# A fused recurrent-attention and expert kernel: the first group's down-projections move behind the second group's attention

## The chip, the cores and the metric

The kernel runs on one core of a Trainium2 chip. The core has five engines that run their own instruction queues in order: TensorE (PE in the profile, with its weight loads as PEld), VectorE (DVE), ScalarE (ACT), GpSimd (POOL) and SyncE (SP), which here only starts DMAs. They meet through semaphores. The metric is the device time of one execution in microseconds. Of the kernel before, three runs took 387.95, 388.36 and 388.54 us; the median is 388.36.

## The reference

Two blocks follow one another. The first is a gated linear recurrence over 768 steps for 4 batches of 8 heads with 48 dimensions:

```python
for t in range(S):
    state = alpha[:, :, t, :, None] * state + np.einsum('bhd,bhe->bhde', k[:, :, t], v[:, :, t])
    y[:, :, t] = np.einsum('bhd,bhde->bhe', q[:, :, t], state)
```

Its output becomes 3072 tokens of 384 values, and goes through an expert block with 1024 hidden values:

```python
h = x @ w_in
h_max = np.max(h, axis=-1, keepdims=True)
e = np.exp(h - h_max)
sm = e / (np.sum(e, axis=-1, keepdims=True) + 1e-09)
solu = h * sm
mu = np.mean(solu, axis=-1, keepdims=True)
var = np.mean((solu - mu) ** 2, axis=-1, keepdims=True)
ln = (solu - mu) / np.sqrt(var + 1e-06) * g_ln
return (ln @ w_out).astype(np.float32)
```

The two weights arrive as 64-bit floats, the rest as 32-bit floats.

## The kernel before

The 768 steps are six groups (g) of 128 steps of all four batches, 512 tokens each. A group goes through three stages.

Attention. Alpha is turned so that time lies along the rows (`alpha_T`, or `turned` on TensorE for the first groups), a backward scan over it gives the decay from a step to the group's end (`scan_back`, tile hT), a forward scan gives the decay from the start (`scan_on`, tile aT, seeded with the inverse of the first). A test that alpha lies in range goes over the same data on ScalarE (`alpha_over`). Keys and queries are multiplied with these decays (`keys`, `queries`), and then scores, masked scores (`masked`, tile sT), the reading of the state (`read_state`), the reading of the values (`read_values`) and the new state (`next_state`) are matmuls and their evictions. `move_lasts` and `move_firsts` bring the queries into the layout of the state by 12 small DMAs, and `decay` multiplies the state by what a group decays it. The tiles of scores, of the transposed keys, of y and of the state's increment all use the four PSUM banks a0 to a3.

Up. For each of eight blocks f of 128 hidden values, three matmuls give h (`up_mm`, PSUM pool of two banks), ScalarE takes its exponential, VectorE the product u = h e, ScalarE the square of u (`up_act`). The sums over the hidden values of e and of u squared are kept by running sums over f (`running`: GpSimd for e, VectorE for the squares); for group 0 they are made on TensorE instead, by matmuls with ones that place four blocks in four quarters of a bank (`array_sums`). `token_sums` turns them into one number for each token. No maximum is subtracted.

Down. For each batch n of a group, four matmuls over f = 0 to 3 and four over f = 4 to 7 (`down(n, half)`), then the normalization from the sums (`finish`). w_out is scaled by g_ln's row, and centred by its column mean (`mean`, `centre`), so that the mean of solu needs no pass of its own. Group 0's downs use w_out before it is centred, and `finish` adds the correction.

The weights come in eight pieces of 64-bit data (0 to 3 of w_in, 4 to 7 of w_out, two blocks f each). `fetch` loads a piece into one of six slots of `room`, `bits` turns it into 32-bit floats by five VectorE steps, `in_range` tests it by two ScalarE passes, and `scaled` multiplies w_out's rows by g_ln on ScalarE. The slots also hold u: three for even groups, three for odd ones, so that a raw piece must be used before u takes its slot.

The order is written out by hand: instructions go to each engine's queue in the order of the program (`tc.manual_schedule`). First group 0's attention (L673 to L710), then a loop over f for group 0's ups with the conversion of pieces 2 to 6 between them (L712 to L742), then a passage with group 0's downs, the rest of the conversion, the mean of w_out and group 1's attention (L743 to L811). From there on each period g does the ups of group g, the downs of group g - 1 (from a list `todo`), and the attention of group g + 1, at places s = 0 to 7 that a table gives (`usual`, and `first` for g = 1, L815 to L826). Before the change `todo` is empty in period 1, and `centres` (L880) puts the centring of w_out at places 4, 6 and 7 of it.

Where a word for the periods is needed: the first period reaches from group 0's first up to group 1's first up, the second from there to group 2's first up, the third to group 3's.

Of the kernel before, what the change touches and what calls it, by code (L numbers as in the profile page):

```python
# [9 lines left out]
FP = mybir.dt.float32  # L10
# [6 lines left out]
P = 128  # L17
# [15 lines left out]
def fast_path(ctx, tc, q, k, v, alpha, moe_w_in, moe_w_out, moe_g_ln, out):  # L33
# [46 lines left out]
    small_ones = const.tile([P, 32], FP, name="small_ones")  # L80
# [33 lines left out]
    seed = [const.tile([P, NP, SW], FP, name=f"seed{i}") for i in range(2)]  # L114
# [95 lines left out]

    def scan_on(g, i):
        part = slice(NP * i, NP * i + NP)
        s = seed[i % 2]
        if i == 2:
            nc.vector.tensor_copy(out=fend[:, g], in_=h4[:, :, 1])

        least = small.tile([P, NP, 1], FP, name="least")
        nc.vector.tensor_scalar(out=least, in0=h4[:, part, 1:2], scalar1=LEAST, scalar2=None, op0=ALU.max)  # L218
        nc.vector.reciprocal(out=s[:, :, 0:1], in_=least)
        scan(aT[:, part], aT[:, part], s, False)  # L220
# [175 lines left out]
    def up_act(g, f):  # L396
        d = gr[g]
        h = d["h"]
        if g:
            e, u2 = (ring.tile([P, T4], FP, name=x) for x in ("e", "u2"))  # L400
        else:
            e, u2 = (sT[:, f % 4, 4 * i : 4 * i + 4].rearrange("p b t -> p (b t)") for i in range(2))
        u = u_of(g, f)
        nc.scalar.activation(out=e, in_=h, func=AF.Exp)  # L404
        nc.vector.tensor_tensor(out=u, in0=h, in1=e, op=ALU.mult)  # L405
        nc.scalar.activation(out=u2, in_=u, func=AF.Square)  # L406
        d[f] = e, u2

    def running(g, f):
# [9 lines left out]
        for i, eng in enumerate((nc.gpsimd, nc.vector)):  # L419
# [4 lines left out]
    def array_sums(g, half):  # L424


        d = gr[g]
        if half == 0:
            d["q"] = [ps_a.tile([P, T4], FP, tag=f"a{i}", name=f"quarters{i}") for i in range(2)]
        for i in range(2):  # L430
            for f in range(4):
                r = quarter(f)
                nc.tensor.matmul(
                    d["q"][i][r], lhsT=ones[:, 0:32], rhs=d[4 * half + f][i], start=half == 0, stop=half == 1,
                    tile_position=(0, r.start), skip_group_check=True,
                )
        if half:
            d["p"] = one.tile([P, 2, T4], FP, name="p")
            for i in range(2):
                nc.scalar.copy(out=d["p"][:, i], in_=d["q"][i])  # L440
            d["unit"] = small_ones
# [6 lines left out]
    def token_sums(g):  # L448
# [3 lines left out]
        t = ps_a.tile([P, B, 2, 32], FP, tag="a3", name="rows") if g else ps_h.tile([P, B, 2, 32], FP, tag="h", name="rows")  # L452
# [131 lines left out]
    def bits(i, part=None):  # L584
        if not float64:
            return
        lo, hi = raws[i][:, :, :, 0], raws[i][:, :, :, 1]
        if part != 1:
            made[i] = [
                lots[2 * (i % 2) + x].rearrange("p (c f) -> p c f", c=hi.shape[1]) for x in range(2)  # L590
            ]
            top = made[i][0].bitcast(U32)
# [6 lines left out]
        if part != 0:  # L599
            top, low = made.pop(i)  # L600
            nc.vector.tensor_scalar(
                out=low.bitcast(U32), in0=top.bitcast(U32), scalar1=0xFF800000, scalar2=None, op0=ALU.bitwise_and
            )
            nc.vector.scalar_tensor_tensor(out=low, in0=lo, scalar=2.0**-52, in1=low, op0=ALU.mult, op1=ALU.mult)
            nc.vector.tensor_tensor(out=place(i), in0=low, in1=top, op=ALU.add)
# [13 lines left out]
    def mean(half):  # L619


        m = ps_h.tile([P, 512], FP, tag="h", name="sums")[:, 0:DM]
# [33 lines left out]
    for s in seed:  # L656
        nc.gpsimd.memset(s, 0.0)
# [6 lines left out]
    nc.vector.memset(small_ones, 1.0 / 32)  # L664
# [16 lines left out]
    alpha_over(0)  # L681
    scan_on(0, 2)
# [28 lines left out]

    for f in range(FC):  # L712
        up_mm(0, f)
        if f == 4:
            array_sums(0, 0)
        up_act(0, f)

        for half in (0, 1) if f == 0 else (f + 1,):
            bits(2 + half // 2, half % 2)
        if f == 0:  # L720
            next_state(0)
            fetch(4, 3)
            load_first(k, kn, 1)
            load_first(q, qn, 1)
            load(alpha, an, 1)
        elif f == 1:
            in_range(2)
        elif f == 2:
            ends_k = ends_of(kn, "e")
        elif f == 3:  # L730
            in_range(3)
            fetch(5, 1)
            fetch(6, 2)
            ends_q = ends_of(qn, "u2")
        elif f == 5:
            in_range(4)
            fetch(7, 3)
            load_v(1)
        elif f == 6:
            scaled(4)  # L740
        elif f == 7:
            scaled(5)  # L742
    bits(6, 1)  # L743
    tk = three("tp_k", [(ps_a, "a2"), (ps_a, "a3"), (ps_h, "h")])
    turned(kn, ends_k, tk)
    load(k, kn, 2)
    array_sums(0, 1)
    down(0, 0)
    scaled(6)
    bits(7)  # L750
    token_sums(0)
    alpha_T(1)
    down(1, 0)
    scaled(7)
    tq = three("tp_q", [(ps_a, "a0"), (ps_a, "a1")])
    turned(qn, ends_q, tq, range(H))
    in_range(5)
    in_range(6)
    for i in range(3):
        scan_back(1, i)  # L760
        part = slice(NP * i, NP * i + NP)
        nc.vector.tensor_tensor(out=kT[:, part], in0=tk[i], in1=hk[:, part], op=ALU.mult)
    mean(0)
    down(0, 1)
    mean(1)
    alpha_over(1)
    load(alpha, an, 2)
# [642 lines left out]
```

## Time and profile before

| what | us |
|---|---|
| median of three runs | 388.36 |
| the profiled execution, its own time | 388.88 |
| its span in the profile | 387.1 |
| first up of group 0 | 32.47 |
| first up of group 1 | 111.87 |
| first up of group 2 | 151.36 |
| first up of group 3 | 206.95 |
| first up of group 4 | 264.12 |

Times in the profile count from the start of the span. In its lists of groups, a line gives the source line, the engine, the operation, the tiles written and read, the shape and the count, then the busy time and the mean of one, then the idle time ahead of it with what ended it. In the timeline a line begins with its start and its length, and merges like instructions that follow one another. Matmuls appear as two records each, since a 32-bit matmul makes two passes. The chain that ended last is only the last output's eviction (VectorE and ScalarE, after 382.34 us), so the reading goes by stretches of time. Clocks are shares of TensorE's full speed that were granted.

### The profile page before, as it was taken

The page shows a single profiled execution, that of the slowest core. Times are in us where ns is not written, and L with a number is a line of the kernel's source. Part 1 is how long each engine was busy: PE and PEld are TensorE (multiplying, and loading weights), DVE is VectorE, ACT ScalarE, POOL GpSimd, SP SyncE. Part 2 cuts the span into 40 slices and gives each one's busy share as a digit, 9 for nine tenths or more (in the row PEclk, how much of TensorE's full clock was granted, in tenths as well). Part 3 has the DMA queues.
Part 4 walks back from the last instruction along what each step waited for, and adds up shares of the span by engine and source line. Part 5 has one row for each costly group of instructions (what it writes and reads, how often), then busy time and mean ns, then how long its engine had stood idle before and what let it go on. Part 6 is the DMA issues. An engine that isn't in the chain of part 4 may idle for free. (4 is left out here: it accounts for less than half of the span.)

```text
span 387.1 us, 10060 instructions
## 1 busy us (share of the span) xinstructions
PE 365.6 (94%) x4341; PEld 219.3 (57%) x4341; DVE 250.7 (65%) x413; ACT 144.5 (37%) x255; POOL 111.5 (29%) x122
## 2 busy tenths in 40 slices
PE   8798899988979998999999999998999999999994
PEld 8685335656645556555557555665556565555652
DVE  0989878996997858885584875664875413444600
ACT  2628566681415426134253153342142132222100
POOL 6000000000232992437130466210475211323200
PEclk9989999999989999999999999999999999999999
DMA  9891978248355535717142627003123000000011
GB/s 182 166 323 51 221 220 200 47 97 183 92 131 104 116 79 102 147 35 161 37 105 47 140 62 172 13 11 70 36 63 89 22 16 8 23 21 20 22 44 47
DMA packets 72439, 36.05 MB, mean 93 GB/s; under 512 B 48185, under 2 KB 69953, under 8 KB 72385
## 3 DMA queue, kind: packets, MB, share of 16 engines
q1 hardware_dynamic: 71360, 34.39, 37.6%
q10 hardware_dynamic: 1024, 0.92, 0.7%
q8 instruction: 36, 0.59, 0.7%
q14 instruction: 19, 0.15, 0.1%
HBM read 25.30 MB, written 4.72 MB: 78 GB/s over the span
## 5 line engine op out<-in xcount | busy, mean ns | idle before, releaser
L390 PE MATMUL h<-x,w_in 128*128 128x512 f32 x288 | 134.8, 608 | 3.4 <-DVE room L405 1.6
L501 PE MATMUL o<-w_out,room 128*128 128x385 f32 x384 | 133.1, 491 | 1.1 <-DVE least L218 1.1
L501 PEld LDWEIGHTS o<-w_out,room 128*128 128x128 f32 x384 | 71.6, 190 | 56.8 <-issue 15.3
L390 PEld LDWEIGHTS h<-x,w_in 128*128 128x128 f32 x288 | 53.1, 192 | 63.5 <-issue 49.2
L405 DVE TENSOR_TENSOR room<-h,e 128x512 f32<-128x512 f32 x40 | 27.7, 693 | 62.6 <-ACT e L404 62.6
L404 ACT ACTIVATE e<-h 128x512 f32<-128x512 f32 x40 | 23.9, 597 | 89.1 <-PE h L390 88.5
L421 POOL TENSOR_TENSOR p<-p,e 128x512 f32<-128x512 f32 x30 | 40.8, 1360 | 21.9 <-ACT e L404 21.5
L406 ACT ACTIVATE u<-room 128x512 f32<-128x512 f32 x40 | 25.2, 630 | 42.5 <-DVE room L405 42.5
L532 POOL TENSOR_TENSOR r<-sums,mhalf 128x1 f32<-128x1 f32 x20 | 12.5, 626 | 91.5 <-DVE sums L524 91.5
L291 DVE TENSOR_TENSOR sT<-a,mask 128x512 f32<-128x512 f32 x44 | 27.3, 683 | 15.3 <-PE a L280 15.3
L280 PE MATMUL a<-qv,kT 32*128 32x128 f32 x704 | 26.2, 289 | 3.9 <-DVE least L218 2.0
L280 PEld LDWEIGHTS a<-qv,kT 32*128 32x128 f32 x704 | 23.2, 196 | 11.0 <-issue 2.3
L421 DVE TENSOR_TENSOR p<-p,u 128x512 f32<-128x512 f32 x30 | 23.6, 786 | 8.4 <-ACT u L406 8.4
L204 DVE TENSOR_TENSOR_SCAN hT<-aT,unit 128x516 f32<-128x516 f32 x18 | 22.3, 1285 | 8.7 <-ACT aT L677 8.6
L204 DVE TENSOR_TENSOR_SCAN aT<-aT,seed 128x516 f32<-128x516 f32 x18 | 25.0, 1391 | 0.6
L329 PE MATMUL y<-sT,vn 128*32 128x128 f32 x768 | 22.6, 273 | 0.4 <-DVE sT L291 0.4
L329 PEld LDWEIGHTS y<-sT,vn 128*32 128x32 f32 x768 | 20.7, 110 | 2.9 <-issue 2.0
L228 POOL TENSOR_TENSOR kT<-kT,hT 128x1024 f32<-128x1024 f32 (+1 forms) x8 | 13.3, 1682 | 29.8 <-DVE kT L179 29.8
L359 ACT COPY x<-y 128x384 f32<-128x384 f32 x24 | 11.2, 480 | 22.7 <-PE y L329 22.7
L196 ACT ACTIVATE sq<-an,mone 128x1536 uint8<-128x1536 f32 x12 | 18.9, 1572 | 0.2
L243 POOL COPY qe<-hT 128x4 f32<-128x4 f32 x5 | 1.0, 191 | 59.4 <-DVE hT L204 59.4
L534 ACT ACTIVATE o_sb<-o,r 128x384 f32<-128x384 f32 x16 | 9.3, 581 | 17.2 <-POOL r L532 17.2
(142 smaller groups left out, 370.2 us busy)
## 6 DMA issues: line engine op xcount, KB each, us to landing
vn<-in_v_dram SPq DMA_DIRECT2D x24, 192.0 KB, 4.5
an<-in_alpha_dram SPq DMA_DIRECT2D x20, 192.0 KB, 4.1
out_dram<-o_sb SPq DMA_DIRECT2D x20, 192.0 KB, 2.0
room<-in_moe_w_in_dram SPq DMA_DIRECT2D x6, 512.0 KB, 7.5
room<-in_moe_w_out_dram SPq DMA_DIRECT2D x8, 384.0 KB, 4.3
kn<-in_k_dram SPq DMA_DIRECT2D x16, 192.0 KB, 3.9
qn<-in_q_dram SPq DMA_DIRECT2D x16, 192.0 KB, 4.7
lot<-qe SPq DMA_DIRECT2D x40, 64.5 KB, 2.1
```

The lines of the kernel that those rows point to most:

```text
L196: nc.scalar.activation(out=sq, in_=x, func=AF.Relu, scale=sign, bias=mone, accum_out=over[:, g, i : i + 1])
L204: nc.vector.tensor_tensor_scan(out=o, data0=a, data1=s, initial=1.0, op0=ALU.mult, op1=ALU.add)
L228: nc.gpsimd.tensor_tensor(out=kT[:, part], in0=kT[:, part], in1=hk[:, part], op=ALU.mult)
L280: nc.tensor.matmul(a[b][:, i], lhsT=kT[quarter(b), kb], rhs=qv[quarter(b), qb, 0:P], start=kb == h, stop=kb != h, tile_position=(32 * b, 0 ...
L291: nc.vector.tensor_tensor(out=sT[:, b, half * NP : half * NP + NP], in0=a[b], in1=mask[:, None, :].to_broadcast([P, NP, P]), op=ALU.mult,)
L329: nc.tensor.matmul(y_bank(b)[quarter(r), a], lhsT=lhsT, rhs=rhs, start=(b, r) not in begun, stop=stop, tile_position=(row, 32 * r), skip_g ...
L390: nc.tensor.matmul(h, lhsT=w_in[:, a, f * P : (f + 1) * P], rhs=d["x"][:, a].rearrange("p b t -> p (b t)"), start=(a == 0), stop=(a == KC ...
L404: nc.scalar.activation(out=e, in_=h, func=AF.Exp)
L405: nc.vector.tensor_tensor(out=u, in0=h, in1=e, op=ALU.mult)
L406: nc.scalar.activation(out=u2, in_=u, func=AF.Square)
L421: eng.tensor_tensor(out=p, in0=d[0][i] if f == 1 else p, in1=d[f][i], op=ALU.add)
L501: nc.tensor.matmul(d["o"][:, 0 : DM + 1], lhsT=u_of(g, f)[:, b * P : b * P + P], rhs=w_out[:, f], start=(f == 0), stop=(f == FC - 1), skip ...
```

## The change

- Group 0's downs leave the passage after the loop. They become the first `todo`, in the order of first halves of two batches, then their second halves, and are done in period 1. The sums and the mean of w_out follow them: `token_sums(0)` at place 0, `mean` at place 2.
- Group 1's keys and queries are turned on TensorE inside the loop over f, and copied from PSUM by ScalarE; their products with the decays are made by GpSimd from SBUF (`keys`, `queries`), not by VectorE from PSUM. Alpha's transposes, backward scans and range test of group 1 stand in the loop too, and the rest of its attention follows without downs.
- Of w_out, piece 4 is converted behind the first scores of group 1, piece 5 behind its state reads, pieces 6 and 7 at places 0 and 1 of period 1. The backward scans of group 3 move from the end of period 1 to place 0 of period 2 (`second`). The centring of w_out is at place 6 of period 1 (rows 0 to 3) and at place 0 of period 2 (rows 4 to 7).
- `bits` works in place in the weight, with one small tile beside it, and its last step is GpSimd's for pieces 3 to 7.
- One reciprocal for all twelve blocks of a group (`inverses`) takes the place of a clamp and a reciprocal for each of three parts; the copy of the group's ends is ScalarE's.
- Group 0's sum of e is a running sum on GpSimd, and its sum of squares a matmul sum after the loop (`array_squares`). Group 1's two running sums are both on GpSimd.

The instructions and transfers before group 0's first up are otherwise the same, except that the loads of group 1's alpha, keys and queries are issued before the loop.

```diff
-    seed = [const.tile([P, NP, SW], FP, name=f"seed{i}") for i in range(2)]
+    seed = const.tile([P, NB, SW], FP, name="seed")
...
+    def inverses(g):
+        nc.scalar.copy(out=fend[:, g], in_=h4[:, :, 1])
+        nc.vector.reciprocal(out=seed[:, :, 0:1], in_=h4[:, :, 1:2])
+
     def scan_on(g, i):
         part = slice(NP * i, NP * i + NP)
-        s = seed[i % 2]
-        if i == 2:
-            nc.vector.tensor_copy(out=fend[:, g], in_=h4[:, :, 1])
-
-        least = small.tile([P, NP, 1], FP, name="least")
-        nc.vector.tensor_scalar(out=least, in0=h4[:, part, 1:2], scalar1=LEAST, scalar2=None, op0=ALU.max)
-        nc.vector.reciprocal(out=s[:, :, 0:1], in_=least)
-        scan(aT[:, part], aT[:, part], s, False)
+        scan(aT[:, part], aT[:, part], seed[:, part], False)
...
-        for i, eng in enumerate((nc.gpsimd, nc.vector)):
+        for i, eng in enumerate((nc.gpsimd, nc.vector if g > 1 else nc.gpsimd)):
+            if g == 0 and i:
+                continue
...
+    def array_squares():
+        d = gr[0]
+        t = ps_a.tile([P, T4], FP, tag="a3", name="quarters")
+        for f in range(FC):
+            r = quarter(f % 4)
+            nc.tensor.matmul(
+                t[r], lhsT=ones[:, 0:32], rhs=d[f][1], start=f < 4, stop=f >= FC - 4,
+                tile_position=(0, r.start), skip_group_check=True,
+            )
+        nc.scalar.mul(out=d["p"][:, 1], in_=t, mul=1.0 / 32)
...
-            nc.vector.tensor_tensor(out=place(i), in0=low, in1=top, op=ALU.add)
+            eng = nc.vector if i < 3 else nc.gpsimd
+            eng.tensor_tensor(out=dst, in0=low, in1=dst, op=ALU.add)
...
     for f in range(FC):
+        up(0, f)
+        if f:
+            running(0, f)
         if f == 0:
+            bits(2, 0)
             next_state(0)
             fetch(4, 3)
         elif f == 1:
+            bits(2, 1)
             in_range(2)
         elif f == 2:
+            bits(3, 0)
+            ends_k = ends_of(kn, 1)
         elif f == 3:
+            bits(3, 1)
+            first_turned(
+                kn, ends_k, [(ps_a, "a0"), (ps_a, "a1"), (ps_a, "a2")], [kT[:, NP * i : NP * i + NP] for i in range(3)]
+            )
             in_range(3)
             fetch(5, 1)
             fetch(6, 2)
+            load_v(1)
+        elif f == 4:
+            alpha_T(1)
+            ends_q = ends_of(qn, 2)
+            load(k, kn, 2)
         elif f == 5:
+            scan_back(1, 0)
+            first_turned(
+                qn, ends_q, [(ps_a, "a3"), (ps_o, "o"), (ps_o, "o")],
+                [qv[:, 0:NP, 0:P], qv[:, NP:H, 0:P], qe[:, :, 0:P]],
+            )
+            load(q, qn, 2)
         elif f == 6:
+            scan_back(1, 1)
+            alpha_over(1)
+            load(alpha, an, 2)
         elif f == 7:
+            scan_back(1, 2)
+    inverses(1)
+    ends_of_decay()
+    keys(1)
     scan_on(1, 2)
+    queries(2)
+    move_lasts()
     apart()
+    array_squares()
+    scan_on(1, 0)
+    queries(0)
+    keys_back(1)
+    scan_on(1, 1)
+    queries(1)
     move_firsts()
     scores(1, 0)
+    bits(4)
+    in_range(4)
+    scaled(4)
+    fetch(7, 3)
     masked(0)
     scores(1, 1)
     masked(1)
+    decay(1)
     read_begin()
     read_state(0)
     read_state(1)
+    bits(5)
+    in_range(5)
+    read_values(1)
+    next_state(1)
+    scaled(5)
+    alpha_T(2)
     alpha_over(2)
     load(alpha, an, 3)
     for i in range(3):
         scan_back(2, i)
+    inverses(2)
...
-        behind={0: "v keys", 1: "on2 on0 on1", 2: "lasts firsts", 3: "apart", 5: "decay", 6: "alpha", 7: "back"},
+        behind={0: "v keys", 1: "on2 on0 on1", 2: "lasts firsts", 3: "apart", 5: "decay", 6: "alpha", 7: "next"},
...
     first = dict(
+        head={4: "keys_back", 5: "masked0", 6: "masked1"},
+        behind={0: "bits6 v keys", 1: "bits7 on2 on0", 2: "on1 lasts", 3: "firsts apart", 5: "decay", 7: "alpha"},
+        tail={2: "mean", 4: "scores0", 5: "scores1", 6: "begin read0", 7: "values"},
         middle={7: "read1"},
     )
+    second = dict(usual, behind={**usual["behind"], 0: "back v keys"})
...
-    centres = {4: (0, 1), 6: (2, 3), 7: (4, 5, 6, 7)}
-    todo = []
+    centres = {(1, 6): range(4), (2, 0): range(4, FC)}
+    todo = [(0, 0), (1, 0), (0, 1), (1, 1), (2, 0), (3, 0), (2, 1), (3, 1)]
...
-            if s == 0 and g > 1:
+            if s == 0:
                 token_sums(g - 1)
```

In the passage after the loop, the lines of the old order that only moved or went are left out of the diff above.

## The prediction

> **What bounds the kernel now.** I read the page's busy shares and slices, then a table of stretches cut at the first matmul of each group, then the timeline around the cuts.
>
> ```profile
> PE 365.6 (94%) x4341; PEld 219.3 (57%) x4341; DVE 250.7 (65%) x413; ACT 144.5 (37%) x255; POOL 111.5 (29%) x122
> ...
> PE   8798899988979998999999999998999999999994
> ...
> DVE  0989878996997858885584875664875413444600
> ```
>
> ```profile
> 32.47:63.50 31.03, 29.43 (x300) 13.48 (x302) 25.39 (x34) 20.19 (x41) 0.00 (x0) 1.00 0.77 190
> 63.50:111.87 48.37, 42.77 (x744) 27.69 (x737) 43.71 (x67) 24.30 (x44) 7.06 (x10) 1.00 0.52 116
> 111.87:151.36 39.49, 37.72 (x581) 22.15 (x573) 30.54 (x42) 17.57 (x31) 23.14 (x24) 0.96 0.41 95
> 151.36:206.95 55.59, 55.59 (x677) 33.01 (x669) 37.77 (x59) 19.43 (x33) 19.85 (x20) 1.00 0.44 97
> ```
>
> Columns of the second: length, then busy time of PE, weight load, DVE, ACT, POOL, clock, DMA. From 151.36 on TensorE never stops: the third period, 55.59 us, is one group's ups, attention and downs back to back. Up to 111.87 VectorE is the bound (43.71 of 48.37) and TensorE's downs stand beside it. The second period has no downs and takes 39.49; without them the third would take 55.59 - 8x2.57 - 0.65 = 34.4 (a half down steps every 2.57 us, the token sums are 0.65), so the second loses 5.1.
>
> ```profile
> 111.65 0.29 PE L367 MATMUL kv<-vn,kg 128*32 128x48 f32 x8 [2.49 <-issue]
> 111.87 9.69 PE L390 MATMUL h<-x,w_in 128*128 128x512 f32 x18
> ...
> 162.04 1.28 POOL L421 TENSOR_TENSOR p<-e 128x512 f32<-128x512 f32 x1
> ...
> 162.44 1.97 DVE L204 TENSOR_TENSOR_SCAN aT<-aT,seed 128x516 f32<-128x516 f32 x1
> ```
>
> Two prices. After a 2.49 us gap 18 up records took 9.69 us, where 427 ns each makes 7.69: a cold clock, 2.0 us. And a scan that alone takes 1.23 took 1.97, because a GpSimd sum held it till 163.3; GpSimd is held likewise (its two sums after 174.86 took 3.08 instead of 2.55). They take turns.
>
> **Bookkeeping.** The change takes 8 half downs (20.6), token sums (0.65) and the mean (1.2) out of the stretch before group 1's first up, and puts them behind it. Call that up's start t1 (now 111.87). With TensorE full, the second period becomes 55.59 + 1.2 = 56.8. Break-even: t1 + 56.8 = 151.36, so t1 = 94.6.
>
> **Start.** One reciprocal instead of three clamps and three reciprocals, and the copy of the ends to ScalarE, save VectorE 0.33, 0.41 and 0.48 us ahead of the scans (13.21 to 13.78, 16.70 to 17.11, 19.44 to 19.92). The query transposes land at 17.6 in any case, so half arrives: first up at 31.85, not 32.47.
>
> **First period.** VectorE loses half of w_out's conversion; ScalarE becomes the queue. From 35.3 it has eight exponentials and squares (8x1.13), two state copies 0.85, six copies of transposed keys and queries (6x0.58), two end copies 1.2, two range tests 4.0, and the alpha test 3.5, which stands ahead of the last exponential: 22.1. Each exponential waits for VectorE's product before its square, 8x0.75 = 6, and two waits for VectorE add some 2.4: last square 65.9, product 65.3. GpSimd takes the running sum of the exponentials (7x1.27) and piece 3's last step; it is idle from 22 to 80 in this trace, and the seventh up wants that piece only some 4 us after it is done. Alpha, keys and queries of group 1 are issued on SP ahead of w_out's pieces, at about 21 to 32, behind all of w_in's: they fit beside a DMA share of 0.30 at 30 to 40, and the pieces behind them wait for free slots in any case (SP waited up to 14.9 us for those).
>
> **Group 1's attention** is then bare: no downs beside it. Keys and queries, which were VectorE products from PSUM (5 or 6 x 0.69), become GpSimd ones: keys 2.18 + 1.18, queries 1.09 + 2x1.21, together 6.9, beside three scans of 1.2 on VectorE. If both run free, the last backward scan ends 66.5, the keys 70.1, the first queries 71.2, then apart 1.35, copy 0.57, four kg copies 1.75: 75. If they take turns, the last backward scan first waits for a sum (67.1), then scan, keys, scan, keys, scan and first queries follow one another from 67.4: 8.1, then the same 3.7: 79.2. Then nothing overlaps, since scores, masks and reads share four PSUM banks: scores 2.07, masks 2.48, scores 2.07, masks 2.48, state reads 2.4, values 3.7, key-values 1.5, hand-overs 0.5: 17.2. The decay needs 12 small DMAs after the queries (7.1 + 2.8 of issue in this trace) and falls just beside it; w_out's piece 7 is fetched behind those DMAs on SP, some 20 us ahead of its use. t1 = 92.2 to 96.4; I take the middle, 94.3: about break-even.
>
> **Second period.** Its second half downs, first wanted right after the third up, need w_out's pieces 6 and 7, whose conversion now stands in the queue behind much. On VectorE after t1: state sums 1.1, alpha's transposes 2.8, three scans 3.4, reciprocal 0.2, ends on ScalarE 0.2, exponential 0.6, product 0.6: 8.9. Token sums 1.1, four bit steps of piece 6 3.1: 13.1. The final sum is now GpSimd's: no row has 768 elements; between 1.24 for 512 and 2.18 for 1024, 1.7. Scaling 1.15: 15.9. ScalarE is in order, so the second exponential waits behind that scaling: 16.5, product 17.1. Piece 7's steps 3.1, sum 1.7, scaling 1.15: 23.1 free, 24.5 taking turns with the keys. TensorE reaches this down after 3 ups, 2 half downs and the token sums, 13.5. Then the mean needs ScalarE between its two matmuls, and ScalarE waits for the third product, behind two scans: 2.3 to 2.9. The bit steps now write in place, into rows 385 apart; the first of them took 0.55 us per piece for w_out and 0.94 for w_in, so it may add 0.4 per piece or nothing; I take nothing, the row of the same piece. Behind the waiting half down stand the mean, the fourth up and, through it, the fourth exponential and all that follows on VectorE. Sum of waits: 8.4 free, 12.0 in turns; 10.2.
>
> **Third period.** w_out's last four rows are centred on GpSimd behind the keys of group 3, and the second half down waits for them. From the first up: product at 4.3, token sums 5.4, backward scans (now here) 8.9, reciprocal, key transposes 11.2, keys 3.36, four centrings 1.03: 18.7 free. The half down was due at 8.6 and ends at 19.4 instead of 11.1: 8.3; in turns with the next scans, four more of 1.2 and 0.67, 12.5. I take 10.4.
>
> **Clock.** Both waits are longer than 2.49, so 2.0 each, 4.0; between 0 and 6 (a third spell in the bare attention). The Trainium skill, "TensorE: Matmul & The Clock Gate", part "HAM oscillation", asks for no idle gap over some 3.4 us; the row above went cold after 2.49. By the page the two long waits would be cold and the mean's gap not: 412.5. By the row the mean's gap could be cold too: 414.5.
>
> **Later.** Same order, TensorE-bound; what VectorE saves there (three clamps of 0.185, two reciprocals of 0.18 and a copy of 0.63, 1.5 us a group) is hidden by TensorE, which has no gap after 151.36 but 2.5 us of its own at 264 and the tail. Group 1's sums of squares on GpSimd (7x1.36) fit: keys 3.4, queries 3.5, decay 1.7, two last bit steps 3.4, fourteen sums 19.0, four centrings 4.1 and four powers 2.2 are 37 of the second period's 67 us. Eight quarter matmuls fewer give nothing, since ScalarE sets that end.
>
> **Sum.** 94.3 + 56.8 + 10.2 - 151.36 = +9.9; third period +10.4; clock +4.0: +24.3. The span 387.1 becomes 411.4; 1.8 lie around it (388.88 - 387.1), and the median of the runs is 0.5 below the profiled one: 412.7, say 412.5. All lows: 92.2 + 56.8 + 8.4 - 151.36 = +6.0, +8.3, +0: 402.7. All highs: +13.8, +12.5, +6: 420.7.
>
> **Rivals.**
> 1. Only one of the two waits exists, because the centring comes in time: 412.5 - 10.4 - 2 = 400. For it: the trace of before has all eight centrings with no wait of TensorE on them. Against: there they stood behind no keys.
> 2. Faster. The conversion keeps pace, TensorE is full from t1 on, and t1 is at its free end: 92.2 + 56.8 - 151.36 = -2.4, so 386. It decides if both waits together are under 2.4 us. For it: VectorE's list in the second period (8 ahead of the first product, products 5.5, bits 6.2, transposes 9.5, scans 3.7, finishes 4.6, masks 5, sums and state 2) is 45 of 57, so capacity is there. Against: the waits come of order, not of load, and the shortest chain to piece 7 is 23 us against 13.5 of TensorE's work.
> 3. GpSimd becomes the bound of the second period: 31 instructions each waiting 0.6 for VectorE's hold bring its 37 to 56, and only from about 67 does it set the end. Price, if it is passed by 5 us: 418. Against: those 11 us of room.
>
> **Chances.** Main case 0.68, rival 1 0.14, rival 2 0.08, rival 3 0.10. Main case and rival 1 span 398 to 421, about 8 in 10, and rival 3 falls inside. This kernel's runs spread 0.15% about the median; under 0.2% is no change. Faster 0.08, same 0.02, slower 0.90.
>
> **What would show it.** Right: TensorE idle some 8 us about 14 us after group 1's first up, waiting for ScalarE's scaling of w_out; idle again in group 2's second half down, waiting for GpSimd's centring; clock near 0.5 after each; t1 near 94; scans over 1.9 us beside GpSimd's keys. Wrong: TensorE busy through both, or t1 under 90. A chain on VectorE that is shorter than I add it, above all bits 6 done before group 1's first product, would break it.

## The result: 7% slower, and where the time went

The changed kernel takes 415.33 us (median of four runs, 413.84 to 417.42) where the kernel before took 388.15 beside it; the ratio is 1.071, 95% interval 1.066 to 1.076. The profiled execution, the fastest of the four, took 413.84, with a span of 412.0. Busy shares, slices and clock, from the page of the changed kernel:

```profile
PE 368.2 (89%) x4325; PEld 221.0 (54%) x4325; DVE 242.5 (59%) x358; ACT 147.9 (36%) x266; POOL 154.9 (38%) x145
...
PE   8789993588829999919999999999999999999995
...
PEclk9999996889969999968999999999999999999999
```

TensorE does the same work as before, but for eight small matmuls, in 25 us more. Its slices show three holes: around 60 to 80, at 112 to 120 and at 175 to 184, each with a lower clock beside it. The table of stretches, cut at TensorE's matmul behind the last square of group 0 and at the first ups of groups 1 to 4 (length, busy time of PE, weight load, DVE, ACT, POOL, then clock, DMA share and GB/s), says what each costs:

```profile
30.60:64.45 33.85, 30.72 (x382) 15.84 (x382) 24.69 (x27) 24.55 (x47) 11.14 (x9) 1.00 0.78 182
64.45:96.71 32.26, 21.31 (x526) 17.49 (x527) 21.43 (x22) 12.99 (x27) 15.65 (x12) 0.79 0.41 95
96.71:166.36 69.65, 60.05 (x693) 34.11 (x687) 43.69 (x56) 27.45 (x50) 37.48 (x33) 0.95 0.35 75
166.36:233.32 66.96, 58.46 (x676) 33.72 (x669) 42.05 (x59) 20.24 (x36) 27.15 (x25) 0.92 0.36 83
233.32:288.91 55.59, 55.59 (x676) 32.98 (x668) 36.77 (x54) 20.02 (x35) 21.31 (x21) 1.00 0.34 78
```

No engine but TensorE is busy for even 70% of the second or third period (VectorE 43.69 of 69.65, GpSimd 37.48), and yet TensorE waits: the two periods are 12.9 and 11.4 longer than full ones of 56.8 and 55.6. TensorE's timeline of the second period shows the first of the two long waits (below, the second wait, after its period):

```profile
111.59 1.56 PE L494 MATMUL o<-w_out,room 128*128 128x385 f32 x4 [0.92 <-ACT w_out L604]
...
120.68 2.93 PE L494 MATMUL o<-w_out,room 128*128 128x385 f32 x4 [7.53 <-ACT w_out L604]
123.54 1.50 PE L618 MATMUL sums<-w_out,ones 128*32 128x384 f32 x16
125.65 0.91 PE L625 MATMUL sums<-o_mean,ones 128*128 128x384 f32 x2 [0.61 <-ACT o_mean L623]
```

The second half down stops at block 6 until ScalarE has scaled w_out's piece 7. In the third period the second half down of its first batch stops likewise, for GpSimd's centring, which stands behind the keys (below, the third wait; TensorE first, then GpSimd):

```profile
183.43 1.65 PE L494 MATMUL o<-w_out,room 128*128 128x385 f32 x2 [8.28 <-POOL w_out L629]
185.30 3.74 PE L494 MATMUL o<-w_out,room 128*128 128x385 f32 x6 [0.22 <-POOL w_out L629]
```

```profile
168.06 0.55 POOL L525 TENSOR_TENSOR r<-sums,mhalf 128x1 f32<-128x1 f32 x1 [6.22 <-DVE sums L517]
177.25 4.24 POOL L224 TENSOR_TENSOR kT<-kT,hT 128x1024 f32<-128x1024 f32 x2 [8.65 <-DVE kT L178]
181.46 5.88 POOL L629 TENSOR_TENSOR w_out<-w_out,mean_sb 128x384 f32<-128x384 f32 x4
```

GpSimd had idled 8.65 ahead of the keys, for VectorE's transposes, with the centring's data there from 160.7 on, when group 0's last down had ended. The other loss is group 1's attention without downs, 64.45 to 96.71, at a clock of 0.79. Its first up is 15.2 earlier than before (96.71 against 111.87), where the prediction's break-even asked for 17.3.

### The profile page after: what moved, and what is told of

Its sections match the earlier page's. It is cut to its first block, busy times and chain, and to the rows that moved or that the text cites. A ratio compares the mean times of both kernels' runs of the same rounds, so it can differ in the third digit from the quotient of the medians.

```text
span 412.0 us, 10021 instructions
## 1 busy us (share of the span) xinstructions
PE 368.2 (89%) x4325; PEld 221.0 (54%) x4325; DVE 242.5 (59%) x358; ACT 147.9 (36%) x266; POOL 154.9 (38%) x145
## 5 line engine op out<-in xcount | busy, mean ns | idle before, releaser
L494 PE MATMUL o<-w_out,room 128*128 128x385 f32 x384 | 136.8, 501 | 16.9 <-POOL w_out L629 8.5
L386 PE MATMUL h<-x,w_in 128*128 128x512 f32 x288 | 133.1, 600 | 1.6 <-DVE w_in L597 0.8
L402 DVE TENSOR_TENSOR room<-h,e 128x512 f32<-128x512 f32 x48 | 33.2, 692 | 91.2 <-ACT e L401 91.2
L401 ACT ACTIVATE e<-h 128x512 f32<-128x512 f32 x48 | 28.5, 594 | 108.0 <-PE h L386 107.5
L420 POOL TENSOR_TENSOR p<-p,e 128x512 f32<-128x512 f32 x36 | 48.5, 1348 | 38.7 <-ACT e L401 38.5
L203 DVE TENSOR_TENSOR_SCAN aT<-aT,seed 128x516 f32<-128x516 f32 x18 | 31.9, 1812 | 0.1
L276 PEld LDWEIGHTS a<-qv,kT 32*128 32x128 f32 x704 | 24.9, 205 | 11.6 <-issue 6.7
L420 POOL TENSOR_TENSOR p<-e 128x512 f32<-128x512 f32 x6 | 10.4, 1730 | 44.5 <-ACT e L401 44.5
L224 POOL TENSOR_TENSOR kT<-kT,hT 128x1024 f32<-128x1024 f32 (+1 forms) x10 | 19.7, 1996 | 19.4 <-DVE kT L178 19.4
L325 PEld LDWEIGHTS y<-sT,vn 128*32 128x32 f32 x768 | 20.7, 110 | 4.3 <-issue 3.1
L420 DVE TENSOR_TENSOR p<-p,u 128x512 f32<-128x512 f32 x24 | 17.7, 739 | 5.8 <-ACT u L403 5.8
L355 ACT COPY x<-y 128x384 f32<-128x384 f32 x24 | 11.1, 479 | 22.5 <-PE y L325 22.4
L597 POOL TENSOR_TENSOR w_out<-lot,w_out 128x768 f32<-128x768 f32 x4 | 7.6, 1893 | 26.7 <-DVE lot L595 26.7
```

Of the source, the lines that this page charges most:

```text
L203: nc.vector.tensor_tensor_scan(out=o, data0=a, data1=s, initial=1.0, op0=ALU.mult, op1=ALU.add)
L224: nc.gpsimd.tensor_tensor(out=kT[:, part], in0=kT[:, part], in1=hk[:, part], op=ALU.mult)
L276: nc.tensor.matmul(a[b][:, i], lhsT=kT[quarter(b), kb], rhs=qv[quarter(b), qb, 0:P], start=kb == h, stop=kb != h, tile_position=(32 * b, 0 ...
L325: nc.tensor.matmul(y_bank(b)[quarter(r), a], lhsT=lhsT, rhs=rhs, start=(b, r) not in begun, stop=stop, tile_position=(row, 32 * r), skip_g ...
L386: nc.tensor.matmul(h, lhsT=w_in[:, a, f * P : (f + 1) * P], rhs=d["x"][:, a].rearrange("p b t -> p (b t)"), start=(a == 0), stop=(a == KC ...
L420: eng.tensor_tensor(out=p, in0=d[0][i] if f == 1 else p, in1=d[f][i], op=ALU.add)
```

## Experiments

Each kernel is the changed one with an edit, but for the two that start from the kernel before. Times are medians; the ratio is to the kernel before, run on the same chip; the last columns are the first ups of groups 0 to 3 in the profiled execution.

| run | us | ratio, 95% interval | 0 | 1 | 2 | 3 |
|---|---|---|---|---|---|---|
| kernel before | 388.15 | 1 | 32.47 | 111.87 | 151.36 | 206.95 |
| changed kernel | 415.33 | 1.066 to 1.076 | 30.60 | 96.71 | 166.36 | 233.32 |
| e1_centre | 404.25 | 1.038 to 1.044 | 31.02 | 98.58 | 169.70 | 225.82 |
| e2_bits | 405.76 | 1.045 to 1.049 | 30.54 | 98.09 | 157.23 | 223.77 |
| e3_both | 394.87 | 1.016 to 1.019 | 32.42 | 100.41 | 159.78 | 215.89 |
| e4_warm | 412.58 | 1.061 to 1.065 | 30.78 | 97.53 | 165.07 | 232.21 |
| e5_psum | 412.09 | 1.059 to 1.068 | 32.05 | 94.97 | 164.81 | 232.48 |
| e6_all | 391.46 | 1.006 to 1.012 | 30.81 | 97.55 | 156.62 | 212.77 |
| e7_recip | 395.60 | 1.015 to 1.024 | 30.70 | 114.18 | 157.15 | 214.06 |
| e8_bare | 414.53 | 1.065 to 1.076 | 30.55 | 94.33 | 166.31 | 234.45 |
| e9_best | 388.70 | 1.001 to 1.006 | 30.39 | 91.14 | 151.47 | 208.19 |
| e10_recip_dve | 385.53 | 0.993 to 0.997 | 30.63 | 110.81 | 148.29 | 203.91 |
| e11_sums | 397.99 | 1.021 to 1.029 | 32.09 | 101.54 | 163.57 | 219.70 |
| e12_ends | 413.82 | 1.064 to 1.071 | 30.44 | 95.97 | 165.86 | 233.25 |

A single profile scatters: where the order is the changed kernel's, the first period took 66.1, 67.6, 66.8 and 65.5 (changed kernel, e1, e4, e12), and the second 69.7 to 71.1. Differences of a stretch under some 1.5 us are not read.

### The third wait: centring ahead of the keys

```diff
+            if g == 2:
+                for f in centres.get((g, s), ()):
+                    centre(f)
             at("behind", s)
-            for f in centres.get((g, s), ()):
+            for f in centres.get((g, s), ()) if g == 1 else ():
                 centre(f)
```

> The changed kernel with one move: the last four centrings of w_out (rows 4 to 7) are issued on GpSimd at place 0 of period 2 ahead of group 3's backward scans and keys, not behind them. The order theory: the third wait is one of queue order alone. GpSimd is idle from 161.8 to 177.3 in the changed kernel but for one power of 0.55, so the four centrings (1.03 each alone) run at about 168.6 to 172.7, and the second half down, due some 9 us after group 2's first up, finds its rows ready. The third period goes from 66.96 to between 55.6 and 58: minus 9 to minus 11.4, time 404 to 406.5. The load theory: the wait only moves, since the keys start later, and with them the products behind the scans: the third period keeps 4 or more of its 11.4, time 408 or above.

11.1 us faster. GpSimd takes the four rows in the hole, and the half down follows its up without a wait (GpSimd, then TensorE):

```profile
171.91 3.60 POOL L629 TENSOR_TENSOR w_out<-w_out,mean_sb 128x384 f32<-128x384 f32 x4
181.45 4.24 POOL L224 TENSOR_TENSOR kT<-kT,hT 128x1024 f32<-128x1024 f32 x2 [5.94 <-DVE kT L178]
```

```profile
175.75 2.74 PE L386 MATMUL h<-x,w_in 128*128 128x512 f32 x6
178.33 2.76 PE L494 MATMUL o<-w_out,room 128*128 128x385 f32 x8
180.92 2.74 PE L386 MATMUL h<-x,w_in 128*128 128x512 f32 x6
```

The third period is 56.1. The keys lose nothing: GpSimd still idles 5.94 ahead of them, for VectorE's transposes. The wait was one of queue order.

### The second wait: conversion ahead of group 1's first up

```diff
     masked(0)
+    decay(1)
+    bits(5)
+    in_range(5)
     scores(1, 1)
     masked(1)
-    decay(1)
...
-    bits(5)
-    in_range(5)
+    bits(6)
+    in_range(6)
+    bits(7)
     read_values(1)
     next_state(1)
-    scaled(5)
+    for i in (5, 6):
+        scaled(i)
+    in_range(7)
+    scaled(7)
...
-        behind={0: "bits6 v keys", 1: "bits7 on2 on0", ...
+        behind={0: "v keys", 1: "on2 on0", ...
```

> The changed kernel with the conversion of w_out's pieces 5 to 7 issued earlier: piece 5 between the two masks of group 1's attention, pieces 6 and 7 behind the second mask, all ahead of group 1's first up; nothing else. The order theory: VectorE waits 3.12 for the second scores and 3.94 for the state's increment in the changed kernel, so bits of pieces 5 and 6 or 7 (3.05 each) fill holes; pieces 6 and 7 are scaled by about 98, before the second half down is due at t1 + 13.5. What stays is the mean's own gap (0.6 to 2.9). The first up of group 1 stays within 1 us of 96.7; the second period goes from 69.65 to between 57 and 60: minus 9.5 to minus 12.5, time 403 to 406. The third wait stays as it was. The load theory (the record's rival 3 among it): VectorE's list ahead of group 1's first product, 8.9, and GpSimd's sums set the period, and a wait for a product takes the place: second period 63 or more, time 408 or above.

9.6 faster, the low end of what the theory of order gave. (The edit also issues `decay(1)` a step earlier.) The half down runs through, and only the mean's gap stays:

```profile
111.89 2.76 PE L494 MATMUL o<-w_out,room 128*128 128x385 f32 x8
114.57 1.50 PE L618 MATMUL sums<-w_out,ones 128*32 128x384 f32 x16
116.68 0.91 PE L625 MATMUL sums<-o_mean,ones 128*128 128x384 f32 x2 [0.61 <-ACT o_mean L623]
```

The second period is 59.1. The steps went into VectorE's waits for the second scores and the state's two increments: 3.12, 3.94 and 1.58 in the changed kernel, nothing, 1.30 and 0.55 here. Group 1's first up is 1.4 later, which is within the scatter. Both moves together:

> Both moves together: centrings ahead of the keys, and pieces 5 to 7 converted ahead of group 1's first up. The order theory: the two gains add: minus 19 to minus 24, time 391.5 to 396.5, which leaves of the change's loss only the late first up of group 1 (96.7 against the break-even at 94.6), 1 to 2 for the mean's gap and up to 3 of products held by GpSimd. The load theory: the gains share one cause and do not add; the time is more than 3 us above the sum of the two single results.

20.5 faster where the two alone sum to 20.7: two separate causes, three quarters of the loss of 27.2. The 6.7 that are left lie ahead of group 1's first up (100.41, where break-even is 94.6) and in the second period, which takes 59.4 for the 56.8 of a full one.

### What the cold clock costs

```diff
+    WN = {0: 28, 4: 32}
...
+            if half and (n, f) in ((0, 6), (4, 4)):
+                warm(WN[n], ps_a, "a0")
```

> The changed kernel with 28 dummy matmuls of 128x128 (ones by ones, about 6 us at full clock) ahead of the sixth block of the second half down of batch 0, and 32 (about 7 us) ahead of the second half down of batch 4: they fill the two waits of 7.5 and 8.3 and change no wait. This measures the clock term of the record, 2.0 for each wait, by itself. If the cold clock behind each wait is a cost of its own, TensorE goes on at full clock behind both: minus 3 to minus 4, time 411.3 to 412.5. If what the cold clock costs is hidden behind the late products that follow, the time stays within 1 of 415.3. If the dummies outlast a wait: up to plus 1.

2.7 faster (412.58; the intervals lie just apart, 1.0653 and 1.0657). TensorE's timeline, the second wait and the third, and the third again as a table of stretches:

```profile
113.84 6.41 PE L439 MATMUL warm<-ones 128*128 128x128 f32 x56
121.52 1.56 PE L498 MATMUL o<-w_out,room 128*128 128x385 f32 x4 [1.27 <-ACT w_out L608]
...
182.23 0.92 PE L498 MATMUL o<-w_out,room 128*128 128x385 f32 x2 [1.22 <-POOL w_out L633]
184.10 3.84 PE L498 MATMUL o<-w_out,room 128*128 128x385 f32 x6 [0.96 <-POOL w_out L633]
```

```profile
182.00:184.00 2.00, 0.92 (x2) 0.30 (x2) 2.00 (x2) 0.00 (x0) 2.00 (x2) 1.00 0.00 0
184.00:186.00 2.00, 1.90 (x3) 1.02 (x4) 0.59 (x1) 0.00 (x0) 2.00 (x3) 0.51 0.00 0
186.00:188.00 2.00, 2.00 (x5) 1.06 (x4) 0.00 (x0) 0.00 (x0) 1.36 (x2) 0.64 0.04 8
```

Behind the second wait four matmuls take 1.56 instead of 2.93, and the period falls from 69.65 to 67.54: the clock term is 2.1 there. Behind the third wait the dummies did not keep the clock. They end at 181.0, two matmuls follow between gaps of 1.22 and 0.96, and then the clock is at 0.51 (the third number from the end of a row). The last six records take 3.84, and the period stays (67.14 against 66.96). So this run does not measure the clock term of the third wait. An estimate from the changed kernel's rows puts it at some 0.8: the last centring ends at 187.34 and the next up starts at 188.87, 1.5 later, where the last two records would take 0.7 at full clock (eight take 2.76); the records before them wait for their centrings at any clock.

```diff
+            if f == FC - 1:
+                warm(12, ps_h, "h")
...
+    warm(15, ps_h, "h")
     keys_back(1)
...
+    warm(14, ps_h, "h")
     scores(1, 0)
```

> The changed kernel with dummy matmuls of 128x128 in the three waits of TensorE in group 1's bare attention: 12 ahead of the last block of the sum of squares (wait 2.84), 15 ahead of the transposed keys (3.57), 14 ahead of the first scores (3.27). It measures what the cold clock costs there, the third spell that the record left at 0 to 6. In the changed kernel the two scores took 4.28 and 5.11 at a granted clock of 0.71 to 0.83, where 2.07 each is the warm price. If the clock is on the path all through: minus 4 to minus 5, time 410.5. If the next wait takes half back (the scores of the second half need the banks of the first masks, and the state's reads need the decay, which in the changed kernel ends at 84.8, 1.3 ahead of the first read): minus 1.2 to minus 3.4, time 412 to 414. If the cold clock there is hidden altogether: 415.

No difference that can be told (414.53). The clock is at 1.00 from 60 to 78, and the first scores take 3.00 instead of 4.28. The second scores take 5.28 (5.11 in the changed kernel): till 80.3 they wait one by one for the first masks, and then the clock is at 0.51 from 81 to 84. So the dummies took only part of this spell away. The first period is 63.8, 1.7 to 3.8 less than in the four profiles above; the second is 72.0, 0.9 to 2.3 more. Whether the second wait took the gain back or the scatter did is not settled.

### Keys and queries of group 1

```diff
-            first_turned(
-                kn, ends_k, [(ps_a, "a0"), (ps_a, "a1"), (ps_a, "a2")], [kT[:, NP * i : NP * i + NP] for i in range(3)]
-            )
+            tk = three("tp_k", [(ps_a, "a0"), (ps_a, "a1"), (ps_a, "a2")])
+            turned(kn, ends_k, tk)
...
-    keys(1)
...
+    for i in range(3):
+        part = slice(NP * i, NP * i + NP)
+        nc.vector.tensor_tensor(out=kT[:, part], in0=tk[i], in1=hk[:, part], op=ALU.mult)
```

and likewise for the queries.

> The changed kernel with one part undone: keys and queries of group 1 are VectorE products straight from PSUM again, as in the kernel before (six of 0.69), so ScalarE loses its six copies (0.57 each) and GpSimd its five products; the order is otherwise that of the change (array_squares goes to a bank of the up's pool). The theory: what made group 1's attention late is the chain of keys and queries in turns, which ends at 76.4 with the copies of kg. Without the copies the last product of group 0 comes 2 to 3 earlier than 63.05, then back scan 1.9, reciprocal 0.2, three products 2.1, three scans and three products 5.8: queries ready at about 70.5. Group 1's first up at 90.5 to 92.5 instead of 96.7, the two waits unchanged: minus 4 to minus 6, time 409 to 411.5. The rival: VectorE, which now carries the products, or the DMAs that bring the queries into the state's layout set the bare attention: first up at 95 or later, time 413.5 or above.

3.2 faster by the medians, less than expected; the two intervals overlap (1.0587 to 1.0675 against 1.0657 to 1.076), and it takes the next run to tell the gain from the scatter. Group 1's first up is at 94.97, not at 90.5 to 92.5. The last product of group 0 comes 31.7 after the first up, not 2 to 3 earlier than 32.5, because the alpha test still stands ahead of the last exponential (in e9_best, where it stands behind, it comes after 30.5). The rest took as long as reckoned: VectorE's scans no longer take turns. First the changed kernel, then this run:

```profile
65.82 6.34 DVE L203 TENSOR_TENSOR_SCAN aT<-aT,seed 128x516 f32<-128x516 f32 x3
```

```profile
68.16 1.22 DVE L203 TENSOR_TENSOR_SCAN aT<-aT,seed 128x516 f32<-128x516 f32 x1
69.48 0.69 DVE L754 TENSOR_TENSOR qe<-tp_q,aT 128x512 f32<-128x512 f32 x1
70.09 1.22 DVE L203 TENSOR_TENSOR_SCAN aT<-aT,seed 128x516 f32<-128x516 f32 x1
```

> Both moves of the wait experiments and the VectorE products from PSUM together. The theory: the three causes are separate and add: 394.9 minus 4 to 6, time 389 to 391, within 0.8% of the kernel before; first up of group 1 near 92 to 95, second and third period 57 to 59.5 and 56. The rival: an earlier first up of group 1 brings the conversion of pieces 5 to 7, which VectorE does behind the masks, onto the path, and half or more of the gain is lost: 392.5 or above.

391.46: 3.4 under the run with both moves, as the single run had 3.2, and here the intervals lie well apart. By the medians the third cause adds too, at its measured size, not at the 4 to 6 expected. The profiles don't show where: the first up of group 1, expected at 92 to 95, is at 97.55, the first period is only 1.3 shorter than in e3_both, which is within the scatter, and another 1.6 are e3_both's late start.

### One reciprocal alone

The kernel before, with `inverses` and the single seed tile, and nothing else of the change:

```diff
-        if i == 2:
-            nc.vector.tensor_copy(out=fend[:, g], in_=h4[:, :, 1])
...
+        nc.scalar.copy(out=fend[:, g], in_=h4[:, :, 1])
+        nc.vector.reciprocal(out=seed[:, :, 0:1], in_=h4[:, :, 1:2])
...
+    inverses(1)
     mean(0)
     down(0, 1)
...
             for i in range(3):
                 scan_back(a + 1, i)
+            inverses(a + 1)
```

> The kernel before with one part of the change alone: one reciprocal for all twelve blocks in place of three clamps and three reciprocals, and the copy of the ends on ScalarE. The record's term: VectorE is 0.33 to 0.48 earlier three times ahead of group 0's scans, half of it arrives: minus 0.6; in the passage up to group 1's first up, where VectorE is busy 43.71 of 48.37, the same part saves 1.5 again, of which up to all arrives: together minus 0.6 to minus 2.1, time 385.7 to 387.2. If the shorter wait also keeps the clock of group 0's first scores (3.39 in the kernel before, 2.08 in the changed one), 1.3 more: down to 384.4. The rival: all of it is hidden by waits for transposes and by TensorE: within 0.2% of 387.8.

7.8 slower, which neither side expected. The start is there (first up of group 0 at 30.70, scores 2.08), but ScalarE, in order, now waits in its queue for all three backward scans. ScalarE's and TensorE's lines, at w_out's mean and at the end of the second period:

```profile
79.60 0.21 ACT L212 COPY fend<-hT 128x12 f32<-128x12 f32 x1 [3.94 <-DVE hT L204]
79.72 0.48 ACT L628 ACTIVATE o_mean<-sums 128x384 f32<-128x384 f32 x1
...
153.57 0.21 ACT L212 COPY fend<-hT 128x12 f32<-128x12 f32 x1 [2.52 <-DVE hT L204]
153.69 1.61 ACT L356 COPY x<-y 128x384 f32<-128x384 f32 x4
```

```profile
80.25 0.91 PE L630 MATMUL sums<-o_mean,ones 128*128 128x384 f32 x2 [3.85 <-ACT o_mean L628]
...
154.22 3.01 PE L364 MATMUL kv<-vn,kg 128*32 128x48 f32 x128 [3.80 <-ACT x L356]
```

TensorE waits 3.85 and 3.80, each with a cold clock behind it (0.50).

```diff
-        nc.scalar.copy(out=fend[:, g], in_=h4[:, :, 1])
+        nc.vector.tensor_copy(out=fend[:, g], in_=h4[:, :, 1])
```

> The kernel before with one reciprocal for all twelve blocks, as in the single run of that part, but the copy of the ends stays on VectorE. In that run ScalarE's copy, which waits for all three backward scans, stood ahead of the scaling of w_out's mean (TensorE waited 3.85 for it) and ahead of group 2's first exponential. If the copy on ScalarE is what cost 7.8, this kernel is back at or below the kernel before: first up of group 0 at 30.6 to 31.9 and 1 saved on VectorE before group 1's first up: 385 to 387.5. If the one reciprocal itself is the cost (it waits for all three scans, and the seeds of all three parts come at once): 391 or above.

With the copy on VectorE the same kernel takes 385.53, ratio 0.995 (0.993 to 0.997): it beats both kernels. A copy of twelve numbers for each row, on the wrong queue, cost 10. In its profile the start is 1.8 earlier, and 1.7 come from the clock, which stays at 1.00 behind a gap of TensorE where the kernel before had 0.50 (18 up records in 7.99 instead of 9.69). Whether the change keeps the clock there or chance does, no run tells.

```profile
110.59 0.29 PE L364 MATMUL kv<-vn,kg 128*32 128x48 f32 x8 [2.58 <-issue]
110.81 7.99 PE L387 MATMUL h<-x,w_in 128*128 128x512 f32 x18
```

The same line of code in the changed kernel:

> The changed kernel with the copy of the ends back on VectorE (the reciprocal stays one for all twelve blocks). Alone on the kernel before, the copy on ScalarE cost 10 (395.6 against 385.5), since ScalarE's queue waited behind it. If the same holds here, the first exponential of group 1, which stands behind the copy (it starts at 103.8, while its up ended at 99.5), comes 4 earlier and the second wait shortens: minus 3 to minus 8, time 407 to 412. If VectorE's queue hides it, since the product behind that exponential stands behind the same three backward scans on VectorE anyway (till 103.7): at most 0.5 earlier, time 414.5 to 415.5, no difference that can be told.

413.82 with an interval that overlaps the changed kernel's: no difference that can be told. The first exponential of group 1 now starts at 98.85, but the product behind it still stands behind the same scans on VectorE, till 103.19.

### The sums on GpSimd

```diff
-        for i, eng in enumerate((nc.gpsimd, nc.vector if g > 1 else nc.gpsimd)):
+        for i, eng in enumerate((nc.gpsimd, nc.vector if g else nc.gpsimd)):
```

> The kernel with both moves, with group 1's running sum of squares back on VectorE (seven adds of 0.69 there for seven of 1.3 on GpSimd). It asks whether the sums on GpSimd cost anything, which the record took as nothing and its rival 3 as 5. If GpSimd has room: 394.9 within 1. If its sums hold back the keys, queries and last steps of that period: minus 1.5 to minus 3. If VectorE is the tighter engine: plus 1 or more.

On the kernel with both moves: 397.99 against 394.87. VectorE is the tighter engine; the mean's gap shows it, since ScalarE's step behind the third product comes later:

```profile
121.65 1.58 PE L625 MATMUL sums<-o_mean,ones 128*128 128x384 f32 x2 [2.13 <-ACT o_mean L623]
123.02 3.81 PE L386 MATMUL h<-x,w_in 128*128 128x512 f32 x6
```

### A version with all of it repaired

Its edits: those of e6_all, piece 4 split around the first mask and pieces 5 to 7 behind the second, dummies in four waits of TensorE, and three steps moved back in their queues (the alpha tests of groups 1 and 2, the last running sum, group 2's backward scans):

```diff
         elif f == 7:
             scan_back(1, 2)
+            alpha_over(1)
     inverses(1)
     ends_of_decay()
+    running(0, 7)
...
+    warm(4, ps_h, "h")
     scores(1, 0)
-    bits(4)
+    bits(4, 0)
     masked(0)
+    decay(1)
+    bits(4, 1)
...
+    warm(9, ps_h, "h")
     scores(1, 1)
     masked(1)
+    warm(5, ps_h, "h")
...
-        behind={0: "bits6 v keys", 1: "bits7 on2 on0", ...
+        behind={0: "range7 back v keys", 1: "on2 on0 over", ...
```

> The attempt at a version that beats both: the centring and the VectorE products of the earlier runs, pieces 5 to 7 converted ahead of group 1's first up but now behind the second mask, piece 4 split around the first mask; dummy matmuls in TensorE's four waits of group 1's attention (24, 4, 9, 5); group 1's alpha test behind the last exponential, the last running sum behind the last backward scan; group 2's backward scans and alpha test behind group 1's first product. Expected from the run with all moves (391.5, first up of group 1 at 97.6, of group 0 at 30.8): the alpha test gives the last product of group 0 back the 2.7 that it waited, the sum 0.6, a mask that no longer waits for piece 4 1.3, and a warm clock (0.50 from 78 to 90 in that run) up to 2: minus 4 to minus 6.5, time 385 to 387.5, even with the kernel before or up to 0.7% below. If the conversion is only pushed into the second half down of period 1, or the clock gives nothing: 388 to 391.

388.70, 0.1% to 0.6% over the kernel before, not the 385 to 387.5 that were expected if all of it came through. TensorE in group 1's attention, at full clock from 60 to 84:

```profile
69.65 2.40 PE L276 MATMUL a<-qv,kT 32*128 32x128 f32 x64
...
74.18 2.47 PE L276 MATMUL a<-qv,kT 32*128 32x128 f32 x64
...
85.41 3.98 PE L325 MATMUL y<-sT,vn 128*32 128x128 f32 x89 [3.35 <-issue]
```

Group 1's first up comes at 91.14, past break-even, but the second period takes 60.3, 3.5 over a full one. A wait of 3.35 that the profile can't name, in the middle of the value reads, takes part of what the clock gave.

## Why the prediction was right

The time (412.5 forecast, 415.3 measured, in the range of 398 to 421), the sign and the two waits came as the main case put them. By its steps:

- **Start.** -0.6 forecast, -1.87 in the profile. The three delays were right; missing was that TensorE's wait ahead of the first scores shrinks from 2.04 to 1.48 with them and the clock stays at 1.00 (scores 3.39 before, 2.08 after). The part alone shows the same (30.63 and 30.70). It does not hold in every execution: three profiles start at 32.05 to 32.42. In e5_psum the wait was 1.97 and the clock 0.50 behind it; in e3_both and e11_sums a wait in the value reads did it (below). TensorE's first scores, before and after:

```profile
19.67 3.39 PE L280 MATMUL a<-qv,kT 32*128 32x128 f32 x64 [2.04 <-DVE least L218]
```

```profile
18.91 2.08 PE L276 MATMUL a<-qv,kT 32*128 32x128 f32 x64 [1.48 <-DVE qv L684]
```

- **First period.** The last square came 33.9 after the first up; 34.1 was forecast. The chain to the end of the copies of the turned-back keys (tile kg) ends at 76.4, 45.8 after the first up, where the prediction had 47.4 in turns and 43.2 free: it was nearer turns, as the held scans show (1812 ns a forward scan on average, 1391 before). The step that failed is the 17.2 for the bare attention: 20.3. Its term of 2.07 for each scores was mis-sized: at a clock of 0.60 and 0.71 they took 4.28 and 5.11, in e9_best at full clock 2.40 and 2.47. Taking the middle between free and turns was a weak choice, since the profile of before already showed turns. That 96.4, the end of the range, meets the 96.71 measured is luck: the start came 1.25 sooner than put, the chain was 1.6 shorter than in turns, the bare attention 3.1 longer. Its two scores in the changed kernel:

```profile
75.51 4.28 PE L276 MATMUL a<-qv,kT 32*128 32x128 f32 x64 [3.27 <-ACT kg L297]
80.47 5.11 PE L276 MATMUL a<-qv,kT 32*128 32x128 f32 x64 [0.68 <-DVE sT L287]
```

- **Second period.** TensorE was ready at t1 + 14.0 (13.5) and piece 7 scaled at t1 + 24.4 (24.5 in turns). Waits of 0.9, 7.5 and 0.6 make 9.1 of the 10.2, and the clock 2.1 of the 2.0. The mean's gap was 0.6, where 2.3 to 2.9 were put; by the prediction's own steps its high end of 12.0 holds that gap (24.5 - 13.5 - 1.3 + 2.3) and its low end of 8.4 does not (23.1 - 13.5 - 1.3). The mean itself was put at 1.2; its matmuls take 1.50 and 0.91 here and took 1.47 and 0.81 before, which is most of what the period has left over. That it is order and not load is shown by e2_bits.
- **Third period.** The half down ended 22.7 after the first up instead of 11.1: 11.6, between the 8.3 and 12.5, near its turns end; the period is 11.4 over. That is already the whole excess: the clock's 2.0 on top of it is not there, since most of it passes while the matmuls wait for their centrings (some 0.8 is left by the estimate above; no run measures it).
- **Clock rule.** The rows here: a gap of 2.04 (before), 1.97 (e5_psum) or 1.99 (e6_all) was followed by a clock of 0.50, one of 1.48 or 1.76 (e6_all, ahead of its first scores) was not; but neither was one of 2.58 (e10_recip_dve). The Trainium skill, "TensorE: Matmul & The Clock Gate", part "HAM oscillation", asks for no gap over some 3.4 us. By that rule the first scores of the kernel before would have been warm, and the start would have gained nothing there. The measurement decides: shorter gaps can bring the cold clock, and their length alone does not tell which do.
- **Later.** No change was forecast; 1.6 came back between groups 3 and 4 (55.59 against 57.17).

The misses cancel in part: group 1's first up 2.4 late, the second period 0.7 over, the third 1.0 under, later 1.6 under: 0.5 together, and the span is 412.0 for 411.4. The rest of the 2.8 to the median is that the profiled execution is 1.5 under it, where that of the kernel before was 0.5 over.

**Rivals.** Rival 1 fell: both waits exist. Rival 2 needed both under 2.4 us; in e9_best, with both gone and the first up at 91.1, the kernel is still no faster than before. Rival 3 fell: GpSimd had 37.5 of 69.7, and taking sums off it made the kernel slower.

## What to carry to other kernels

When work moves, list for every queue what now stands ahead of what, and when each result is due: here engines with 40% of idle time gave two waits of 8 us, and two moves of a few lines took 20 of 27 us back. A small instruction that waits for late data holds everything behind it on an in-order engine, so put it on the engine that makes the data. A part of a change is worth running alone: this one held a gain of 0.5% that the rest hid.

## What the runs showed of the hardware

- TensorE's clock fell after shorter gaps than the 2.49 that the prediction knew: 1.97 to 2.04, not after 1.48 or 1.76. But it did not fall after 2.58 in e10_recip_dve. In the clock records of these traces each cold stretch except the one at the end of the span lasts 3.41 us or a multiple of it (3.41 behind the first scores of the kernel before, 6.83 and 10.24 from the two long waits of the changed one), so the clock is set in steps. Whether a gap's place in such a step decides, no run here tests. Two shorter gaps close together brought the cold clock too. In group 0's value reads, e11_sums had 0.81 and 1.12, and 0.50 at 27 to 29; e10_recip_dve 0.81 and 1.02, and 1.00 all through (TensorE's timelines, in this order):

```profile
24.18 0.63 PE L325 MATMUL y<-sT,vn 128*32 128x128 f32 x13 [0.81 <-DVE sT L287]
25.93 4.71 PE L325 MATMUL y<-sT,vn 128*32 128x128 f32 x103 [1.12 <-issue]
```

```profile
24.31 0.63 PE L326 MATMUL y<-sT,vn 128*32 128x128 f32 x13 [0.81 <-DVE sT L288]
25.96 3.04 PE L326 MATMUL y<-sT,vn 128*32 128x128 f32 x103 [1.02 <-issue]
```

  In these two profiles a tenth of a microsecond went with 1.5 of the start. The three late starts of the table (e3_both, e5_psum, e11_sums) each had such a spell.
- GpSimd's add of 768 elements takes 1.68 alone and up to 2.5 beside VectorE's scans. VectorE's three products with an operand in PSUM took 1.82 beside a GpSimd sum (e9_best) and 1.82 without one (e6_all): there neither held the other.
- Runs of a hundred and more small matmuls stop for 0.4 to 3.4 us with no releaser (2.49 before, 1.79 after, 3.35 in e9_best). No run here tells why.
